# An attention, slot-expert and feed-forward kernel: a written order for the expert stage, and its constants loaded in parts over ScalarE's queue

## The chip, the cores and the metric

The program runs on one core of one Trainium2 chip. The metric is the device time of one execution in microseconds, lower is better. The times shown for the kernel before are the median and the ends of 3 runs. One further execution was profiled, and every row below comes from it.

## What is computed

Three layers in a chain, on 4 batches of 576 tokens with 512 features, all in float32:

```
attn = g * phi(q) M / (phi(q) z) + (1 - g) * softmax(causal(q k^T / 8)) v      # 8 heads of 64
logits = x @ phi                        # x = attn as 2304 x 512; 8 experts of 4 slots: 32 slots
d = softmax over the tokens(logits);  slot_input = d^T @ x
slot_out[e] = max(slot_input[e] @ w1[e], 0) @ w2[e]      # w1 512 x 1024, w2 1024 x 512, e = 0..7
y = softmax over the slots(logits) @ slot_out
out = (s * max(y @ w_in, 0)^2 + b) @ w_out               # w_in 512 x 2048, w_out 2048 x 512
```

The two arrays `w_in` and `w_out` arrive as float64 and are decoded on the chip.

## The kernel before, in words

**Attention.** 16 pairs of heads. What TensorE, ScalarE, VectorE and GpSimd do for them is one written order, the table `STEP`: each word is a part of a pair's work and the number of pairs it runs ahead. The first things that each pair needs are its keys (`load_keys`, L276) and its queries, values and memory (`load_rest`, L282). The scores are a matmul into PSUM (L308), the row maxima with the causal mask added are a VectorE instruction (L320 and L326), which reads the mask from the tile `cs`, and the exponentials are ScalarE's (L334). Transposes (L353) read the identity from `cs` as well. `cs` holds four things side by side: identity (128 columns), the mask for the first four blocks of rows (512), the mask for the last block (288), and a replication matrix `rep` (128), which is first read when the softmax over the tokens is finished. In each pair's iteration a piece of `w_in` is loaded into `raw` (L572) and decoded, the first step on ScalarE (L201).

**Loads.** All are issued by SyncE, in order. Eight semaphores serve them in turn, so each issue waits until the load eight places before has landed. `bet` (beta, from which ScalarE makes `eb` at L616 and L617 and VectorE `icst` at L620 and L623) and `cs` are among the first. Expert weights (33.5 MB) are loaded during the attention into all tiles that are free, as units of 512 columns, and into the tiles of the attention as it ends: `load_place`, `load_next`, and `used`, which refills a tile when its weights have been read.

**Experts.** Four experts stand in the 4 column groups of TensorE at once, so there are two halves, `a` = 0 and 1. `layer1(a)` multiplies the slots by `w1` (L664), takes the maximum with 0 on ScalarE into `hs` (L669), transposes it (L674) and copies it to `hT` (L220). `layer2(a)` multiplies by `w2` (L684) and copies to `so`. `slots_T(a)` transposes `so` (L697) into `sT`. `slot_softmax(b)` is the softmax over the slots for batch b: ten VectorE instructions and one of ScalarE (L744 to L753), five transposes (L758, L761) and two copies into `cT`. Its results `cex`, `chi` and `csk` stand in one buffer each for all batches. The tile `hs` lies in `raw64`, `hT` in `PT`, and `csk` in `F`; all three hold expert weights until these have been read. In this stage the framework's scheduler chooses the order on each engine.

**Feed-forward.** A written order again, `RAMP`, for the start: `g_piece` builds `slot_out @ w_in` (L789, L793, L797), `decode_part` decodes `w_out` (L201 to L209, L720, L722), `first` (L826 to L846) and `second` (L861) are the two matmuls with what lies between. Then follows the main loop.

Of the kernel before, what the change touches and what calls it, by code (L numbers as in the profile page):

```python
# [27 lines left out]
C_ID = 0  # L28
# [22 lines left out]
    kw=[0,0,0,0,0],  # L51
# [18 lines left out]
scl:2 U2.1:2 Wd:2 du:0 F1:3 pscl:2 C:1 A:1 E3.0:2 M:2 T0.1:3 T4.1:2 A4:1 U0.1:3  # L70
""".split()
# [19 lines left out]
def tile_attention_moe_ffn(  # L91
# [40 lines left out]
    ONCE = ("w1", "w2", "w3", "raw", "M", "x", "raw64", "F", "PT", "Q0", "Q1")  # L132
# [17 lines left out]
    wt, left = {}, []  # L150
# [13 lines left out]
    def load_place(n, tag):  # L164
# [4 lines left out]
        if n % 2 and (left or wkeys):  # L169
            if not left:  # L170
                left.extend([k] for k in wkeys.pop(-1 if tag == "x" else 0))
            keys.append(left.pop(0))
# [334 lines left out]
    def merge(part):  # L507
# [147 lines left out]
    hs, so = MB[:, 0:1024], MB[:, 1152:1664]  # L655
# [3 lines left out]
    def layer1(a):  # L659
        acc = [ps_y(), ps_y()]  # L660
        for kc in range(4):
            for fb in range(2):
                for j in range(4):
                    PE.matmul(  # L664
                        acc[fb][32 * j:32 * j + 32, :], slT[:, kc, :], wt["w1", a, kc, j, fb],
                        start=(kc == 0), stop=(kc == 3))
# [3 lines left out]
        for g in range(2):  # L670
            t = ps_h()
# [3 lines left out]
            evac(hT[a][:, 4 * g:4 * g + 4, :], t.rearrange("p (i s) -> p i s", i=4))  # L675

    def layer2(a):

        n = UNIT // (1 + a)
        acc = [ps_y() for _ in range(1 + a)]  # L680
        for fc in range(8):
            for i, y in enumerate(acc):
                for j in range(4):
                    last_pe[0] = PE.matmul(  # L684
# [4 lines left out]
        for i, y in enumerate(acc):  # L689
            evac(so[:, n * i:n * i + n], y[:, 0:n], ("a", "v")[i] if a else None)  # L690

    def slots_T(a):
        t = ps_h()
        if a:
            keep_warm(t, T["kw"][1])
        for dc in range(4):
            PE.transpose(t[:, dc * 128:(dc + 1) * 128], so[:, dc * 128:(dc + 1) * 128], ident)  # L697
        evac(sT[:, :, 16 * a:16 * a + 16].rearrange("p c (j s) -> p c j s", j=4),
             strided(t[:, 16 * a:16 * a + 1], (128, 4), (36, 4), (1, 4)), "v" if a else None)
# [28 lines left out]

    layer1(0)
    layer1(1)  # L730
    layer2(0)
    slots_T(0)
    load_out(0)

# [29 lines left out]
    for b in range(2):  # L764
        slot_softmax(b)
# [194 lines left out]
```

## Time and profile before

| | us |
|---|---|
| median of 3 runs | 511.17 |
| fastest and slowest of them | 508.05, 513.64 |
| the profiled execution | 512.23 |
| its span, first to last instruction | 510.4 |
| TensorE busy in it | 486.8 |

The profiled execution spends 1.8 us outside its span. All rows below are on the span's own clock, which begins with the first instruction. PE is TensorE's matmul, PEld its load of weights, DVE VectorE, ACT ScalarE, SPq SyncE's queue of issues. A float32 matmul stands in the trace as two records.

### The profile page before, as it was taken

How to read it: one execution, taken by the hardware profiler on the slowest of the kernel's cores; microseconds unless marked ns; L12 is line 12 of the kernel's file. 1: busy time of each engine (PE TensorE's matmuls, PEld its weight loads, DVE VectorE, ACT ScalarE, POOL GpSimd, SP SyncE). 2: the span in 40 equal slices, each digit the busy share in tenths (PEclk: the TensorE clock that was granted, in tenths of full speed). 3: DMA queues.
4: the chain of work that ended last, by engine and by line, in shares of the span. 5: the costliest groups of instructions: out<-in, count | busy, mean ns of one | idle time of the engine just before them, and what ended most of it. 6: DMA issues, size and time to landing. Idle time of an engine off the chain costs nothing.

```text
span 510.4 us, 8982 instructions
## 1 busy us (share of the span) xinstructions
PE 486.8 (95%) x3143; PEld 344.5 (67%) x3143; DVE 340.4 (67%) x934; ACT 334.3 (65%) x843; POOL 57.2 (11%) x73
## 2 busy tenths in 40 slices
PE   2999999999999999988998999999999999999997
PEld 1566665666566656763344667888888888888885
DVE  0888897888788878842226899984644655645451
ACT  2888876888788887720124799887766555566552
POOL 1122222222223312300000000000000000000000
PEclk9999999999999999998999999999999999999999
DMA  7689995344434442499997542500300100100101
GB/s 243 209 304 323 359 367 162 114 147 147 148 99 148 145 141 78 147 377 403 409 408 252 211 163 85 166 1 1 123 2 0 62 2 0 63 1 17 45 2 62
DMA packets 25821, 78.28 MB, mean 153 GB/s; under 512 B 3120, under 2 KB 3248, under 8 KB 25776
## 3 DMA queue, kind: packets, MB, share of 16 engines
q1 hardware_dynamic: 25776, 77.71, 43.7%
q8 instruction: 25, 0.41, 0.3%
q14 instruction: 20, 0.16, 0.1%
HBM read 69.84 MB, written 7.86 MB: 152 GB/s over the span
## 4 chain that ended last, share of the span: by engine, by line
PE 88%; DMA 6%; DVE 2%; ACT 2%; issue 1%; SPq 1%; DVEq 0%; ACTq 0%
PE y L861 39%; PE t L353 8%; PE o L402 8%; PE s L308 8%; PE s L312 3%; PE h L826 3%; PE s L373 3%; PE y L684 3%; DMA w<-in_w_dram 3%; PE t L356 2%; DMA cs<-in_cst_dram 2%; PE t L414 1%; DMA raw<-in_w_in_dram 1%; PE t L437 1%; PE t L450 1%; PE h L789 1%
## 5 line engine op out<-in xcount | busy, mean ns | idle before, releaser
L861 PE MATMUL y<-w,R 128*128 128x512 f32 x864 | 215.3, 393 | 0.7 <-ACT R L838 0.7
L861 PEld LDWEIGHTS y<-w,R 128*128 128x128 f32 x864 | 160.6, 188 | 37.1 <-issue 2.4
L830 ACT ACTIVATE P<-h 128x384 f32<-128x384 f32 x96 | 46.5, 485 | 55.1 <-PE h L826 54.8
L320 DVE CUSTOM_DVE_ANT_0 P<-s,cs 128x128 f32<-128x128 f32 (+3 forms) x128 | 58.3, 481 | 28.5 <-DMA cs<-in_cst_dram 11.2
L334 ACT ACTIVATE P<-P,st 128x128 f32<-128x128 f32 (+3 forms) x128 | 71.2, 557 | 0.4
L846 DVE TENSOR_TENSOR R<-P,R 128x384 fp32r<-128x384 f32 x47 | 26.1, 556 | 66.7 <-ACT R L844 66.6
L353 PE MATMUL t<-cs,P 128*128 128x128 f32 x320 | 54.2, 285 | 0.0
L353 PEld LDWEIGHTS t<-cs,P 128*128 128x128 f32 x320 | 34.8, 141 | 19.5 <-ACT P L334 6.3
L308 PE MATMUL s<-R,Q 64*128 64x128 f32 (+3 forms) x176 | 32.5, 476 | 10.8 <-DVE st L320 5.6
L222 ACT ACTIVATE PT<-t 128x256 f32<-128x256 f32 (+2 forms) x64 | 26.0, 433 | 13.8 <-PE t L353 13.8
L826 PE MATMUL h<-x,R 128*128 128x384 f32 x96 | 34.1, 356 | 0.5 <-DVE R L797 0.5
L836 ACT ACTIVATE P<-P,sbt 128x384 f32<-128x384 f32 x47 | 33.3, 708 | 1.4
L842 DVE SCALAR_TENSOR_TENSOR R<-P,sbt,R 128x384 fp32r<-128x384 f32 x49 | 30.1, 617 | 5.1 <-ACT R L838 2.1
L834 DVE SCALAR_TENSOR_TENSOR P<-P,sbt 128x384 f32<-128x384 f32 x49 | 29.9, 612 | 0.9 <-ACT P L830 0.9
L222 ACT ACTIVATE raw<-t 128x256 f32<-128x256 f32 (+2 forms) x64 | 25.8, 432 | 6.6 <-PE t L353 6.5
L308 PEld LDWEIGHTS s<-R,Q 64*128 64x128 f32 x176 | 15.5, 194 | 20.3 <-issue 10.6
L844 ACT ACTIVATE R<-P 128x384 fp32r<-128x384 f32 x47 | 24.6, 523 | 1.3
L832 ACT ACTIVATE P<-P 128x384 f32<-128x384 f32 x47 | 24.6, 523 | 1.3
L334 ACT ACTIVATION_READ_ACCUMULATOR P<-P,st 128x1 f32 x128 | 24.9, 195 | 0.0
L347 POOL TENSOR_SCALAR P<-P,st 128x576 f32<-128x576 f32 x16 | 16.1, 1008 | 65.0 <-DVE st L343 51.7
L826 PEld LDWEIGHTS h<-x,R 128*128 128x128 f32 x96 | 17.9, 188 | 6.3 <-DVE R L797 1.4
L431 POOL TENSOR_TENSOR x<-x,M 128x512 f32<-128x512 f32 x15 | 19.2, 1279 | 9.8 <-DVE x L425 8.6
(237 smaller groups left out, 748.7 us busy)
## 6 DMA issues: line engine op xcount, KB each, us to landing
w<-in_w_dram SPq DMA_DIRECT2D x38, 512.0 KB, 8.1
raw<-in_w_in_dram SPq DMA_DIRECT2D x16, 512.0 KB, 4.2
Q<-in_qvm_dram SPq DMA_DIRECT2D x10, 673.0 KB, 4.3
R<-in_qk_dram SPq DMA_DIRECT2D x32, 144.0 KB, 3.3
out_dram<-P SPq DMA_DIRECT2D x18, 256.0 KB, 2.0
PT<-in_w_out_dram SPq DMA_DIRECT2D x4, 1024.0 KB, 5.0
R<-in_qvm_dram SPq DMA_DIRECT2D x5, 673.0 KB, 4.4
wdr<-raw SPq DMA_DIRECT2D x12, 256.0 KB, 2.2
```

What stands on the lines that cost most here:

```text
L222: ACT.activation(out=dst, in_=src, func=AF.Copy)
L308: PE.matmul(ps[:, 512 * h:512 * h + n], q[r, t * 128:(t + 1) * 128], k[r, 0:n], start=True, stop=True)
L320: DVE.tensor_tensor_reduce(out=Pt[h, t], in0=x, in1=cs[:, C_M2 - n:C_M2], scale=-0.125, scalar=BIG, op0=ALU.add, op1=ALU.min, accum_out=st ...
L334: ACT.activation(out=pt, in_=pt, func=AF.Exp, scale=-1.0, bias=st[:, 18 + c:19 + c], accum_out=st[:, c:c + 1])
L353: PE.transpose(tp[:, kb * 128:(kb + 1) * 128], Pt[i, t][:, kb * 128:(kb + 1) * 128], ident)
L402: last_pe[0] = PE.matmul(o[64 * h:64 * h + 64, q0 - 64:512], lhs(kb, h), PTp[:, h, c:c + S - q0], start=(kb == 0), stop=(kb == 4))
L826: PE.matmul(g_t[n][2], G(k * 128, 128), cT[:, g * TG:(g + 1) * TG], start=True, stop=True)
L830: ACT.activation(out=r, in_=h, func=AF.Relu)
L834: DVE.scalar_tensor_tensor(out=r, in0=r, scalar=sbt[:, 0:1], in1=r, op0=ALU.mult, op1=ALU.mult)
L836: ACT.activation(out=r, in_=r, func=AF.Identity, scale=sbt[:, 0:1], bias=sbt[:, 1:2])
L842: DVE.scalar_tensor_tensor(out=lo, in0=r, scalar=sbt[:, 1:2], in1=hi, op0=ALU.add, op1=ALU.subtract)
L861: PE.matmul(acc[g, i], (hi, hi, lo)[j][:, c], (who, wlo, who)[j][k], start=(k == 0 and j == 0), stop=(k == NK - 1 and j == 2))
```

## The change

1. `bet` and `cs` are issued from ScalarE's queue, ahead of all else there, `cs` in four parts in this order: the last 128 columns of the first mask, the identity, the other 384 columns of that mask, the second mask. SyncE starts with the keys of pair 0. `phs`, `sbt` and the replication matrix are issued by SyncE at the end of the iteration before the first full one.
2. The expert stage has a written order for TensorE, ScalarE and VectorE, the table `EXPERTS`. A word is a part and its arguments: `1a.from.to` and `2a.from.to` are pieces of the two layers, `r` the maximum with 0, `h` the transposes (part 0) and the copies (part 1), `o` the copy of the second layer's result, `T` the slots' transposes, `c` the softmax (part 0 its VectorE and ScalarE instructions, part 1 transposes and copies), `w` the load of the first part of `w_out`.
3. The maximum with 0 is shared: ScalarE takes the first 512 columns, VectorE the others. The copies have named engines.
4. `hs` and `so` move to `R2`, which is no longer refilled with weights. The softmax of batch 1 has buffers of its own in the tile `raw`. The loads of half pairs are limited to six, so that the last weights stand in other tiles.
5. `keep_warm` calls with a count of 0 are removed.

```diff
-    load_keys(0)
-    load_rest(0)
-    SP.dma_start(out=cs, in_=cst)
-    SP.dma_start(out=bet, in_=beta)
-    SP.dma_start(out=phs, in_=phi)
-    SP.dma_start(out=sbt, in_=sb)
+    ACT.dma_start(out=bet, in_=beta)
+    for c in (slice(C_M2 - 128, C_M2), slice(C_ID, C_M1), slice(C_M1, C_M2 - 128), slice(C_M2, C_REP)):
+        ACT.dma_start(out=cs[:, c], in_=cst[:, c])
+    load_keys(0)
+    load_rest(0)
...
+            if i == -1:
+                SP.dma_start(out=phs, in_=phi)
+                SP.dma_start(out=sbt, in_=sb)
+                SP.dma_start(out=cs[:, C_REP:C_END], in_=cst[:, C_REP:C_END])
...
+EXPERTS = """
+10.0.4 11.0.1 r0 11.1.2 h0.0 11.2.4 h0.1 r1 c0.0 20.0.4 h1.0 h1.1 20.4.8 o0 c0.1 c1.0
+21.0.2 T0 21.2.4 c1.1 21.4.6 w0 21.6.8 o1
+""".split()
...
-    hs, so = MB[:, 0:1024], MB[:, 1152:1664]
+    RB = place("R2", SIZE["R2"])
+    hs, so = RB[:, 0:1024], RB[:, 1024:1536]
...
-        for fb in range(2):
-            ACT.activation(out=hs[:, fb * 512:(fb + 1) * 512], in_=acc[fb], func=AF.Relu)
+    def layer1_out(a):
+        ACT.activation(out=hs[:, 0:512], in_=acc1[a][0], func=AF.Relu)
+        DVE.tensor_scalar(out=hs[:, 512:1024], in0=acc1[a][1], scalar1=0.0, scalar2=-BIG, op0=ALU.max, op1=ALU.max)
...
-    layer1(0)
-    layer1(1)
-    layer2(0)
-    slots_T(0)
-    load_out(0)
...
-    for b in range(2):
-        slot_softmax(b)
-
-    layer2(1)
+    parts = {"1": layer1, "r": layer1_out, "h": hidden_T, "2": layer2, "o": layer2_out, "T": slots_T, "c": slot_softmax, "w": load_out}
+    with tc.manual_schedule(engines={mybir.EngineType.PE, mybir.EngineType.Activation, mybir.EngineType.DVE}):
+        for word in EXPERTS:
+            a = [int(i) for i in word[1:].split(".")]
+            if word[0] in "12":
+                a = [a[0], range(a[1], a[2])]
+            parts[word[0]](*a)
```

**ScalarE at the program's start.** Before, its first work is the load of the function table and the two exponentials of `bet`:

```order
L616 ACT_TABLE_LOAD
L616 ACTIVATE eb<-bet 128x12
L617 ACTIVATE eb<-bet 128x12
L334 ACTIVATE P,st<-P,st 128x128
L290 ACTIVATE F<-F 128x576
```

Now five issues of loads stand ahead of these:

```order
L615 DMA bet<-in_beta_dram 128x12
L617 DMA cs<-in_cst_dram 128x128 x2
L617 DMA cs<-in_cst_dram 128x384
L617 DMA cs<-in_cst_dram 128x288
L622 ACT_TABLE_LOAD
L622 ACTIVATE eb<-bet 128x12
```

The loads went from SyncE's queue to ScalarE's, and what ScalarE computes stands behind them. On VectorE the nine small instructions on `eb` and `icst` now stand ahead of the first maximum instead of behind it.

**TensorE from the end of layer 1 to the begin of layer 2.** `y<-...,slT` is layer 1, `h<-cs,...` transposes of `hs`, `y<-...,PT` layer 2 of the first half. Before:

```order
L664 MATMUL y<-PT,slT 32x512 x2
L674 MATMUL h<-cs,raw_2788 128x128 x8
L664 MATMUL y<-PT,slT 32x512 x2
L664 MATMUL y<-P,slT 32x512
L664 MATMUL y<-PT,slT 32x512 x2
L664 MATMUL y<-R_2660,slT 32x512
L664 MATMUL y<-P,slT 32x512
L674 MATMUL h<-cs,raw_2788 128x128 x4
L684 MATMUL y<-P,PT 32x512
L674 MATMUL h<-cs,raw_2788 128x128 x4
L684 MATMUL y<-P,PT 32x512
```

Now:

```order
L696 MATMUL h<-cs,R_2792 128x128 x8
L678 MATMUL y<-raw_2569,slT 32x512 x2
L678 MATMUL y<-Q_2574,slT 32x512
L678 MATMUL y<-PT,slT 32x512
L678 MATMUL y<-raw_2569,slT 32x512 x2
L678 MATMUL y<-Q_2574,slT 32x512
L678 MATMUL y<-PT,slT 32x512 x4
L678 MATMUL y<-P,slT 32x512
L678 MATMUL y<-PT,slT 32x512 x2
L678 MATMUL y<-R_2664,slT 32x512
L678 MATMUL y<-P,slT 32x512
L708 MATMUL y<-P,PT 32x512 x2
```

The first half's transposes stand half of `layer1(1)` earlier, and the second half's, which stood between the first two matmuls of layer 2, come 16 matmuls later.

**VectorE before the transposes of batch 1.** `x<-h` copies the transposed softmax of batch 0, `raw` and `raw_2790` are the buffers of batch 1 and of batch 2. It now has this stretch, up to the two last rows, which finish what the transposes of batch 1 read:

```order
L231 CAST x<-h 128x512 [waits DMAHW3_49,DMAHW2_49,PE_49]
L775 TENSOR_REDUCE raw<-lgs 128x5 [waits DMAHW6_49,DMAHW5_49,DMAHW4_49]
L783 CAST F<-raw_2790 128x10x32 [waits DVE_49,PE_49]
L776 TENSOR_TENSOR raw<-lgs,raw 128x160 [waits DVE_49]
L784 TENSOR_TENSOR F<-raw_2790 128x10x32
L778 TENSOR_REDUCE raw<-raw 128x5 [waits Activation_49]
L776 TENSOR_TENSOR raw_2790<-lgs,raw_2790 128x160 [waits DVE_49]
L779 TENSOR_SCALAR raw<-raw 128x5 [waits DVE_49]
L780 RECIPROCAL raw<-raw 128x5 [waits DVE_49]
L781 TENSOR_TENSOR raw<-raw 128x160 [waits DVE_49]
```

```order
L778 TENSOR_REDUCE raw_2790<-raw_2790 128x5 [waits Activation_49]
L782 CAST raw<-raw 128x160 [waits DVE_49]
L779 TENSOR_SCALAR raw_2790<-raw_2790 128x5 [waits DVE_49]
L783 CAST raw<-raw 128x10x32 [waits DVE_49]
L784 TENSOR_TENSOR raw<-raw 128x10x32
```

Between the copy for batch 0 and the last instruction for batch 1 stand 14 instructions, of which five belong to batch 2. Before, batch 1 shared its buffers with batch 0, and its last two instructions on `F` could only follow the transposes of batch 0.

## Rows read from the trace of the kernel before

**Rows 1.** The page's chain that ended last, share of the span by engine.

```profile
PE 88%; DMA 6%; DVE 2%; ACT 2%; issue 1%; SPq 1%; DVEq 0%; ACTq 0%
```

**Rows 2.** That chain in order of time: start us, us, what.

```profile
3.08 7.95 DMA cs<-in_cst_dram
...
71.02 7.24 DMA raw<-in_w_in_dram
```

**Rows 3.** Timeline of the start: start us, us, engine, line, what [idle before, releaser].

```profile
0.73 1.28 ACT L616 ACT_TABLE_LOAD   x1 [0.73 <-PEq L950]
...
3.08 0.43 SPq L610 DMA_DIRECT2D cs<-in_cst_dram  x1
...
5.24 1.66 PE L308 MATMUL s<-R,Q 64*128 64x128 f32 x8 [5.24 <-DMA Q<-in_qvm_dram]
...
8.88 0.33 SPq L572 DMA_DIRECT2D raw<-in_w_in_dram  x1
...
11.17 0.29 DVE L320 CUSTOM_DVE_ANT_0 P<-s,cs 128x128 f32<-128x128 f32 x1 [11.17 <-DMA cs<-in_cst_dram]
11.31 0.21 ACT L616 ACTIVATE eb<-bet 128x12 f32<-128x12 f32 x1 [9.29 <-DMA bet<-in_beta_dram]
...
17.24 0.68 ACT L201 ACTIVATE win<-raw 128x512 f32<-128x512 f32 x1
```

**Rows 4.** Windows of the start: busy us per engine; last PEclk, DMA share, GB/s.

```profile
2.00:4.00 2.00, 0.00 (x0) 0.00 (x0) 0.00 (x0) 0.01 (x1) 0.00 (x0) 1.00 0.81 205
4.00:6.00 2.00, 0.77 (x6) 0.80 (x8) 0.00 (x0) 0.00 (x0) 0.67 (x1) 1.00 0.95 322
6.00:8.00 2.00, 0.89 (x5) 0.17 (x2) 0.00 (x0) 0.00 (x0) 0.00 (x0) 1.00 1.04 309
8.00:10.00 2.00, 0.00 (x0) 0.00 (x0) 0.00 (x0) 0.00 (x0) 0.00 (x0) 1.00 0.97 373
10.00:12.00 2.00, 0.26 (x2) 0.26 (x4) 0.83 (x7) 0.59 (x3) 0.00 (x0) 1.00 0.92 244
```

**Rows 5.** Timeline of the expert stage, TensorE and ScalarE.

```profile
236.86 8.77 PE L664 MATMUL y<-w,slT 128*32 128x512 f32 x64 [0.45 <-DVE slT L650]
...
247.17 0.13 PEld L664 LDWEIGHTS y<-w,slT 128*32 128x32 f32 x4 [0.30 <-issue]
247.60 0.13 PEld L664 LDWEIGHTS y<-w,slT 128*32 128x32 f32 x4 [0.30 <-issue]
...
250.87 1.09 ACT L669 ACTIVATE raw<-y 128x512 f32<-128x512 f32 x2 [17.24 <-DMA w<-in_w_dram]
...
254.65 0.59 ACT L220 COPY PT<-h 128x512 f32<-128x512 f32 x1
...
265.38 0.66 PE L697 MATMUL h<-cs,raw 128*128 128x128 f32 x4 [0.27 <-ACT raw L220]
...
266.60 4.73 PE L684 MATMUL y<-w,PT 128*32 128x256 f32 x82
...
274.71 0.38 ACT L222 ACTIVATE raw<-y 128x256 f32<-128x256 f32 x1 [0.28 <-PE y L684]
...
276.30 0.64 PE L789 MATMUL y<-win,raw 128*32 128x128 f32 x16 [0.32 <-DVE raw L224]
```

**Rows 6.** Timeline of VectorE, first and last of nine softmax instructions in a row.

```profile
266.71 0.49 DVE L752 COPY F<-raw 128x320 f32<-128x320 f32 x1 [8.40 <-PE h L761]
...
269.50 0.25 DVE L751 CAST raw<-raw 128x160 fp32r<-128x160 f32 x1
```

**Rows 7.** Windows of the expert stage, columns as in rows 4 (third busy time is VectorE's).

```profile
236.00:240.00 4.00, 3.55 (x24) 1.24 (x27) 0.29 (x1) 0.00 (x0) 0.00 (x0) 0.71 1.03 405
268.00:272.00 4.00, 4.00 (x80) 2.71 (x77) 1.56 (x6) 0.33 (x1) 0.00 (x0) 1.00 1.00 384
272.00:276.00 4.00, 3.51 (x34) 1.58 (x25) 1.90 (x6) 2.37 (x6) 0.00 (x0) 1.00 0.12 46
280.00:284.00 4.00, 3.35 (x15) 2.83 (x16) 3.93 (x10) 3.29 (x6) 0.00 (x0) 1.00 1.04 404
```

More of the change, by code (lines that the diff above doesn't have):

```diff
@@ L50 @@
     sim=0,
-    kw=[0,0,0,0,0],
     sb=[30, 34],
@@ L149, in tile_attention_moe_ffn @@
     at = {k: i for i, k in enumerate(k for pair in wkeys for k in pair)}
-    wt, left = {}, []
+    wt, left, odd = {}, [], [6]
     def load_units(keys, dst):
@@ L168, in load_place @@
         keys = [wkeys.pop(0) for _ in range(min(n // 2, len(wkeys)))]
-        if n % 2 and (left or wkeys):
+        if n % 2 and odd[0]:
+            odd[0] -= 1
             if not left:
-                left.extend([k] for k in wkeys.pop(-1 if tag == "x" else 0))
+                left.extend([k] for k in wkeys.pop(0))
             keys.append(left.pop(0))
@@ L654, in tile_attention_moe_ffn, with layer1 @@
     HB = place("PT", SIZE["PT"])
-    hs, so = MB[:, 0:1024], MB[:, 1152:1664]
+    RB = place("R2", SIZE["R2"])
+    hs, so = RB[:, 0:1024], RB[:, 1024:1536]
     sT = MB[:, 1024:1152].rearrange("p (c s) -> p c s", c=4)
     hT = [HB[:, 1024 * i:1024 * i + 1024].rearrange("p (f s) -> p f s", f=8) for i in range(2)]
-    def layer1(a):
-        acc = [ps_y(), ps_y()]
-        for kc in range(4):
+    acc1, acc2 = {}, {}
+    def layer1(a, kcs):
+        if a not in acc1:
+            acc1[a] = [ps_y(), ps_y()]
+        for kc in kcs:
             for fb in range(2):
@@ L674, in layer1, with layer2 @@
                 PE.transpose(t[:, i * 128:(i + 1) * 128], strided(hs[:, c:c + 1], (2, 128)), ident)
-            evac(hT[a][:, 4 * g:4 * g + 4, :], t.rearrange("p (i s) -> p i s", i=4))
-    def layer2(a):
+    h_t = {}
+    def layer2(a, fcs):
         n = UNIT // (1 + a)
-        acc = [ps_y() for _ in range(1 + a)]
-        for fc in range(8):
-            for i, y in enumerate(acc):
+        if a not in acc2:
+            acc2[a] = [ps_y() for _ in range(1 + a)]
+        for fc in fcs:
+            for i, y in enumerate(acc2[a]):
                 for j in range(4):
-                    last_pe[0] = PE.matmul(
+                    PE.matmul(
                         y[32 * j:32 * j + 32, 0:n], hT[a][:, fc, 32 * j:32 * j + 32],
@@ L688, in layer2, with layer2_out @@
                 used(8)
-        for i, y in enumerate(acc):
-            evac(so[:, n * i:n * i + n], y[:, 0:n], ("a", "v")[i] if a else None)
+    def layer2_out(a):
+        n = UNIT // (1 + a)
+        for i, y in enumerate(acc2[a]):
+            evac(so[:, n * i:n * i + n], y[:, 0:n], "av"[i])
     def slots_T(a):
         t = ps_h()
-        if a:
-            keep_warm(t, T["kw"][1])
         for dc in range(4):
@@ L727, in decode_out, with slot_softmax @@
         load_out(k2 + 2)
-    layer1(0)
-    layer1(1)
-    layer2(0)
-    slots_T(0)
-    load_out(0)
     XC = place("x", SIZE["x"], F32R)
     cT = XC
-    csk = place("F", SIZE["F"]).rearrange("p (t r s) -> p t r s", t=5, r=4)
-    c5 = MB[:, 1984:1994]
-    cex, chi = (MB[:, 1664 + 160 * i:1824 + 160 * i].rearrange("p (t s) -> p t s", t=5) for i in range(2))
-    chi = chi.bitcast(F32R)
-    def slot_softmax(b):
+    CB = place("raw", SIZE["raw"])
+    csks = [place("F", SIZE["F"]), CB[:, 0:640]]
+    cexs = [MB[:, 1664:1994], CB[:, 640:970]]
+    def slot_softmax(b, part, by="va"):
+        i = b % 2 if b < 2 else 0
+        csk = csks[i].rearrange("p (t r s) -> p t r s", t=5, r=4)
+        if part:
+            t, t2 = ps_h(), ps_h()
+            for i in range(4):
+                PE.transpose(t[:, i * 128:(i + 1) * 128], csk[:, i].rearrange("p r s -> p (r s)"), ident)
+            PE.transpose(t2[:, 0:64], csk[0:64, 4].rearrange("p r s -> p (r s)"), ident[0:64, 0:64])
+            evac(cT[:, b * S:b * S + 512], t, by[0])
+            evac(cT[:, b * S + 512:(b + 1) * S], t2[:, 0:64], by[1])
+            return
+        c5 = cexs[i][:, 320:330]
+        cex, chi = (cexs[i][:, 160 * r:160 * r + 160].rearrange("p (t s) -> p t s", t=5) for r in range(2))
+        chi = chi.bitcast(F32R)
         DVE.tensor_reduce(out=c5[:, 0:5], in_=lgs[:, b], axis=AX.X, op=ALU.max)
@@ L786, in g_piece @@
         if part == 0:
-            keep_warm(t, T["kw"][2] if i == 0 else 0)
             for dc in range(4):
```

30 lines of the change are left out of this document (13 added, 17 removed).

## The prediction

> **What bounds the kernel now.** I read the chain that ended last first, since it says whose time is worth anything. TensorE has 88% of it and loads 6% [rows 1]; so an edit pays where the chain leaves TensorE, or where TensorE's own order leaves it idle. In order of time the chain leaves it first at the very start: from 3.08 us, for 7.95 us, it is the load of the constants [rows 2]. The timeline there shows why: pair 0's scores begin at 5.24, the first maximum only at 11.17, freed by that load, and the exponential of `bet` stands 9.29 us for its own [rows 3]. Then I went to the two stages that the change reorders. Between 236.86, where layer 1 begins, and 276.30, where the first window matmul of the feed-forward begins, lie 39.4 us [rows 5].
>
> **Term 1, the constants at the start.** Nothing is computed less; loads change queue and order. Before the first maximum the changed kernel needs pair 0's keys and queries, the first 128 columns of mask, and nine small VectorE instructions on `eb`, which wait for ScalarE. ScalarE: five issues at 0.43 us, the price of one on SyncE's queue [rows 3], from 0.73 make 2.9; the table load of 1.28 makes 4.2; two exponentials at 0.21 make 4.6. The nine small ones, narrower than the softmax instructions of rows 6 (0.34 each) and by estimate half as long, end near 6.0 [rows 6]. This is hidden by the queries if these come later, and costs little if not.
>
> The queries landed for 5.24 with nothing beside them but SyncE's loads. Now 481 KB from ScalarE's queue (128 rows of 128 + 128 + 384 + 288 + 12 words) may go ahead of them; at 322 GB/s [rows 4] that is 1.5 us at most. So scores begin between 5.24 and 6.7. The first two of their eight records take 0.4 us of 1.66 [rows 3]. First maximum between 5.7 and 7.2; I take 6.9, near the late end, as the engines that move data are already 81 to 95% busy in this stretch [rows 4]. It stood at 11.17, so the start moves by 4.3 us, at best by 5.5.
>
> The other end comes from how late a landing is told. By bytes, the constants (541 KB, behind 984 KB of keys, queries and values) had passed by 7.5 us: 0.41 MB by 4, 1.05 by 6, 1.67 by 8 [rows 4]. VectorE was freed at 11.17, 3.6 us later. If such a lag falls on pair 0's queries or the first mask, the first maximum stands at 10.4 and the gain is 0.8.
>
> What is late next: the first piece of `w_in`, which ScalarE reads at 17.24 without a wait that shows [rows 3]. Its 524 KB follow 2.58 MB of the loads ahead of it. 2.91 MB had passed by 12 [rows 4], and the other 0.2 MB take 0.8 us at 244 GB/s, so by bytes it ended near 12.8, and with the lag of 3.6 near 16.4. Now 131 KB less stand ahead (the replication matrix and `phs` are moved behind), 0.5 us. It then lands between 12.3 and 15.9, and is wanted at 17.24 less 4.3, 12.9. The middle is 14.1, so ScalarE may stand 1.2 us with exponentials queued behind it, for which TensorE's transposes wait. I take 0.5 of it as lost, for scores of the next pair stand ahead of those transposes. **Term 1: 3.8 us gained, bounds 0.8 and 5.5.**
>
> The Trainium skill ("Trainium Kernel Development and Optimization", section Key Constraints) says that loads issued from several queues run on the same 16 engines and interleave, and that a second queue only saves issue time. By that rule the gain from the queue itself is SyncE's issues alone, and the constants would cost the queries the whole 1.5 us. The busy share of 0.95 [rows 4] agrees; what is left is the order of need.
>
> The three loads put into SyncE's queue two pairs later (130 KB) are issues of 0.43 us each beside work that does not need them.
>
> **Term 2, the expert stage.** TensorE's work is the same; I add it up in the written order. A group of four records of 512 columns starts every 0.43 us [rows 5], so 0.1075 each: 128 records of layer 1 are 13.8, 64 of `layer2(0)` 6.9. 256 columns cost 4.73 / 82 = 0.058, with its end; steady 0.0535, half of 0.1075: 128 records are 6.9. Four transposes are 0.66 [rows 5]; two sets of eight, three sets of four and two single ones make 5.0. The first 64 records take 8.77 where 6.9 would do [rows 5], as the granted clock is 0.71 there, a mean of a part at 1.2 and a part at 2.4 GHz [rows 7]; what precedes is unchanged, so the 1.9 stay. Sum 34.5.
>
> Then the waits. The maximum with 0, which stood 17.24 us because `hs` lay in a tile of weights [rows 5], now finds `R2` free after the first quarter of `layer1(1)`, beside TensorE's next 16 records: hidden. The copy into `PT` must still wait for the last of layer 1, as `PT` holds its weights; 0.59 for it [rows 5] and 0.1 for passing on, 0.7 on the path. The new wait is `c1.1`: its transposes need 14 VectorE instructions behind the copy for batch 0. Nine such took 3.04 us, 266.71 to 269.75 [rows 6], so 14 take 4.7. The copy for batch 0 (0.6) starts as its four transposes end, so the buffer is ready 5.3 us after these. TensorE meanwhile has one single transpose (0.2), `21.0.2`, `T0` and `21.2.4`: 0.2 + 1.7 + 0.7 + 1.7 = 4.3. With the passing on it stands about 1.2. Queued behind is all that is left of layer 2, 3.4 us, and nothing fills the gap.
>
> 34.5 + 0.7 + 1.2 = 36.4 from 236.86: layer 2 ends at 273.3, against 274.71 when ScalarE copies its result [rows 5]: 1.4 gained. After it two copies now start together, where VectorE's came later, as it was at work on a softmax: 0.2 more. **Term 2: 1.6 us, bounds 0** (the wait at `c1.1` grows to 2.8, as VectorE's chain passes through ScalarE twice) **and 2.8** (it is hidden).
>
> The weights bound it next. The load engines are full to 272 and idle after it [rows 7]; the last 2 MB they move are `w_out` and a window, 5 us at 384 to 405 GB/s, so the last weights land by 267, and the new order wants them from 271. Hidden, unless the wait at `c1.1` goes: then the margin is under 3.
>
> **Term 3, the ramp.** Six softmax instructions of batch 2 that stood behind the expert stage are now inside it. VectorE is busy 3.93 of 4 us at 280 [rows 7]; six at 0.34 are 2.0, of which I take 0.5, since TensorE waits for VectorE there only now and then. **Bounds 0 and 0.9.** The `keep_warm` calls had a count of 0: nothing.
>
> **Sum.** 3.8 + 1.6 + 0.5 = 5.9. The profiled execution took 512.23: 506.3. The median of the runs is 1.06 lower, which would give 505.3. I take 505.8, between them.
>
> **The rivals.**
>
> - *The start gains little.* The lag of 3.6 us falls on the queries or the mask: term 1 is 0.8, time 508.8. For it: the lag is there in the trace, of a cause that no row shows. Against: the queries themselves came without it, 0.59 MB with the keys by 5.24 [rows 3].
> - *VectorE is in time at `c1.1`, and `w_in` is not late.* 1.2 and 0.5 more: 504.1. For it: five of the 14 instructions fill pauses of dependent ones, so the mean from rows 6 may be high. Against: the nine that it comes from were mixed in the same way.
> - *The start's gain is spent later.* The chain hangs for 7.24 us on a load of `w_in` at 71.02 [rows 2], while the engines that load are full. If that load's landing is fixed by bytes since the start, the 3.8 turn into a longer wait: 509.6. Against: each such issue waits for a buffer that the engines free, so the stream moves with them.
> - *Slower: the clock falls at the new wait.* TensorE stands at `c1.1`, and the ramp behind has its own gaps. If the granted clock falls there to 1.2 GHz and stays through the ramp, to 292, some 22 us in which TensorE is busy about half at its limit cost 11: 517. It decides from a loss of 5.9 us of full-speed work; the dip at 236 [rows 7] cost 1.9. Against: 272 to 276, with half a microsecond of pauses, were granted 1.00 [rows 7].
>
> The Trainium skill ("TensorE: Matmul & The Clock Gate", section "HAM oscillation — how this bites in real kernels") tells of a matmul kernel that lost the clock at each wait for data; by that rule this rival is the result. Only the 0.71 at 236 [rows 7] speaks for it here.
>
> **How the numbers follow.** Forecast 0.60; little at the start 0.15; in time at `c1.1` 0.12; spent later 0.08; slower 0.05. The bounds of the terms are 0.8 and 9.2 gained; from 511.17 that is 510.4 and 502.0, and the forecast's own part 503.5 to 507.5. The range, 501.8 to 510.5, spans these; it leaves out the slower rival and some 0.1 for what is larger at the start than its bounds. About 1%, 5.1 us, is what a measurement here can tell: below 506.1 lie 0.42 of the forecast's 0.60, all of the second rival and a little of the others: faster 0.57, same 0.38, slower 0.05.
>
> **What would show it.** First maximum at 6.9 and no wait for constants; ScalarE's first read of `raw` near 13.5 with a wait for its load; from layer 1 to the first window matmul 37.8 us instead of 39.4, with a wait of TensorE of about 1.2 for VectorE at the transposes of batch 1; the granted clock at 1.00 after it. It is wrong if the first maximum stands later than 9, if the stretch from 60 to 82 grew, or if layer 2 stands still for weights.

## The result and the profile after

The changed kernel took 507.09 us (median of 7 runs, 502.12 to 509.79), the kernel before 511.35 beside it (7 runs, 508.05 to 513.64): a ratio of 0.989, 95% interval 0.985 to 0.994. In a second set of runs (the tenth experiment) it was 0.993 (0.990 to 0.996). The medians are of all runs and the ratios of the fast ones alone: one of these 7 runs, and four of the 12 in the second set, were over 1.5% above the fastest and count as slow. The forecast was 505.8. The profiled execution of the changed kernel took 506.75, with a span of 504.9, 5.5 less than before.

The page has the chain by engine, which answers to [rows 1]:

```profile
PE 91%; DMA 4%; DVE 2%; ACT 1%; issue 0%; SPq 0%; DVEq 0%; ACTq 0%
```

The chain in order of time leaves TensorE for loads at these three places only; the constants and the `raw` of [rows 2] are gone from it. Through the last two TensorE is busy all the same, so only the first is a pause:

```profile
1.97 3.86 DMA Q<-in_qvm_dram
...
240.24 9.34 DMA w<-in_w_dram
...
252.16 7.66 DMA P<-in_w_dram
```

The timeline of the start, for [rows 3] (start us, us, engine, line, what):

```profile
1.14 2.01 ACTq L617 DMA_DIRECT2D cs<-in_cst_dram  x4
3.18 1.28 ACT L622 ACT_TABLE_LOAD   x1 [3.18 <-issue]
4.47 0.21 ACT L622 ACTIVATE eb<-bet 128x12 f32<-128x12 f32 x1
...
5.41 0.44 SPq L578 DMA_DIRECT2D raw<-in_w_in_dram  x1
...
5.96 3.06 PE L315 MATMUL s<-R,Q 64*128 64x128 f32 x12 [5.96 <-DMA Q<-in_qvm_dram]
...
6.80 0.29 DVE L327 CUSTOM_DVE_ANT_0 P<-s,cs 128x128 f32<-128x128 f32 x1 [1.11 <-PE s L315]
...
12.87 0.67 ACT L208 ACTIVATE win<-raw 128x512 f32<-128x512 f32 x1
```

The first maximum stands at 6.80 instead of 11.17 and waits for TensorE's scores, not for the constants; the scores wait for the load of the queries. ScalarE reads the first piece of `w_in` at 12.87 without a wait. The expert stage, for [rows 5], on three engines:

```profile
232.00 9.37 PE L678 MATMUL y<-w,slT 128*32 128x512 f32 x64 [0.45 <-DVE slT L660]
...
243.16 0.60 ACT L684 ACTIVATE R<-y 128x512 f32<-128x512 f32 x1 [15.15 <-PE y L678]
...
249.56 0.60 ACT L229 ACTIVATE PT<-h 128x512 f32<-128x512 f32 x1 [5.80 <-DMA w<-in_w_dram]
250.21 0.62 PE L708 MATMUL y<-P,PT 128*32 128x512 f32 x2 [0.68 <-ACT PT L229]
...
259.81 0.31 DVE L775 TENSOR_REDUCE raw<-lgs 128x5 f32<-128x160 f32 x1
...
261.75 1.93 PE L708 MATMUL y<-w,PT 128*32 128x256 f32 x32
...
263.18 0.48 DVE L784 TENSOR_TENSOR raw<-raw 128x320 f32<-128x320 f32 x1
...
263.81 0.63 PE L767 MATMUL h<-cs,raw 128*128 128x128 f32 x4
...
267.92 0.38 ACT L229 ACTIVATE R<-y 128x256 f32<-128x256 f32 x1 [3.03 <-PE y L708]
268.30 0.42 DVE L231 COPY R<-y 128x256 f32<-128x256 f32 x1 [3.13 <-PE y L708]
269.53 0.64 PE L815 MATMUL y<-win,raw 128*32 128x128 f32 x16 [0.32 <-DVE raw L231]
```

From layer 1 (232.00) to the first window matmul (269.53) it is 37.5 us instead of 39.4. The maximum with 0 runs at 243.16, in the middle of layer 1, where it stood until 250.87. The windows, for [rows 7] (busy us by engine; last the granted clock, DMA share, GB/s):

```profile
228.00:232.00 4.00, 2.33 (x11) 1.99 (x11) 1.57 (x5) 0.01 (x1) 0.00 (x0) 0.73 1.03 402
232.00:236.00 4.00, 4.00 (x20) 0.99 (x24) 0.00 (x0) 0.00 (x0) 0.00 (x0) 0.50 0.88 348
236.00:240.00 4.00, 4.00 (x40) 1.13 (x36) 0.00 (x0) 0.00 (x0) 0.00 (x0) 0.92 0.89 301
...
268.00:272.00 4.00, 2.90 (x32) 1.59 (x26) 2.88 (x7) 2.41 (x7) 0.00 (x0) 1.00 0.73 246
272.00:276.00 4.00, 2.91 (x15) 1.86 (x15) 3.51 (x8) 3.23 (x7) 0.00 (x0) 0.78 1.03 386
276.00:280.00 4.00, 4.00 (x16) 3.27 (x15) 2.95 (x6) 1.87 (x4) 0.00 (x0) 0.80 0.48 194
```

The granted clock falls to 0.50 (1.2 GHz) ahead of layer 1, and part of two windows behind the stage is at that level as well.

The 5.5 us come about so: the shift against the kernel before is 4.4 at the first maximum and 5.6 from pair 7 on, 4.9 at layer 1, 6.8 at the first window matmul, and 5.5 from 286 us to the end.

### The profile page after: what moved, and what is told of

The parts are those of the page before. It is cut to its first block, busy times and chain, and to the rows that moved or that the text cites. A ratio compares the mean times of both kernels' runs of the same rounds, so it can differ in the third digit from the quotient of the medians.

```text
span 504.9 us, 8984 instructions
## 1 busy us (share of the span) xinstructions
PE 487.1 (96%) x3143; PEld 344.9 (68%) x3143; DVE 343.0 (68%) x939; ACT 331.6 (66%) x838; POOL 57.4 (11%) x73
## 4 chain that ended last, share of the span: by engine, by line
PE 91%; DMA 4%; DVE 2%; ACT 1%; issue 0%; SPq 0%; DVEq 0%; ACTq 0%
PE y L885 40%; PE s L315 8%; PE t L360 8%; PE o L409 8%; PE s L319 4%; PE s L380 4%; PE h L851 3%; DMA w<-in_w_dram 2%; PE t L363 2%; PE t L421 2%; PE y L678 2%; DMA P<-in_w_dram 2%; PE t L444 1%; PE t L457 1%; PE y L708 1%; PE t L404 1%
## 5 line engine op out<-in xcount | busy, mean ns | idle before, releaser
L871 DVE TENSOR_TENSOR R<-P,R 128x384 fp32r<-128x384 f32 x47 | 26.1, 556 | 66.4 <-ACT R L869 66.3
L327 DVE CUSTOM_DVE_ANT_0 P<-s,cs 128x128 f32<-128x128 f32 (+3 forms) x128 | 58.3, 480 | 18.8 <-ACT PT L229 9.0
```

Source lines behind the costliest of these rows:

```text
L327: DVE.tensor_tensor_reduce(out=Pt[h, t], in0=x, in1=cs[:, C_M2 - n:C_M2], scale=-0.125, scalar=BIG, op0=ALU.add, op1=ALU.min, accum_out=st ...
```

## The experiments

Each ran beside the kernel before, on the same chip as it. A ratio is to that kernel, with its 95% interval. Where times in one execution are compared, they are starts read from the timelines: the first maximum of a pair, the first record of layer 1, the first window matmul.

| kernel | median us | ratio | interval |
|---|---|---|---|
| start alone | 509.88 | 0.998 | 0.995 to 1.001 |
| start alone, again | 508.30 | 0.995 | 0.994 to 0.997 |
| experts alone | 508.09 | 0.996 | 0.995 to 0.998 |
| changed kernel, again | 508.51 | 0.993 | 0.990 to 0.996 |
| scheduler's order | 508.72 | 0.996 | 0.993 to 0.998 |
| pauses filled | 506.33 | 0.991 | 0.989 to 0.993 |
| one queue | 510.74 | 1.000 | 0.997 to 1.003 |
| weights spread | 514.01 | 1.005 | 1.003 to 1.007 |
| weights spread, pauses filled | 513.13 | 1.003 | 1.002 to 1.005 |
| weights behind `raw` | 506.89 | 0.991 | 0.987 to 0.994 |
| weights behind `raw`, pauses filled | 507.08 | 0.990 | 0.986 to 0.994 |

| execution | first maximum | pair 2 | pair 7 | layer 1 | first window matmul |
|---|---|---|---|---|---|
| before | 11.17 | 28.67 | 94.98 | 236.86 | 276.30 |
| before, again | 9.15 | 27.47 | 92.90 | 234.83 | 274.02 |
| experts alone (old start) | 8.84 | 27.10 | 94.63 | 236.51 | 273.44 |
| changed | 6.80 | 24.36 | 89.34 | 232.00 | 269.53 |
| changed, again | 8.18 | 25.34 | 90.90 | 232.87 | 269.81 |
| start alone | 7.38 | 24.46 | 92.76 | 234.68 | 274.11 |
| start alone, again | 7.67 | 24.74 | 90.83 | 232.75 | 272.19 |
| pauses filled | 7.20 | 24.61 | 90.75 | 233.02 | 270.73 |
| scheduler's order | 8.36 | 26.11 | 91.48 | 234.00 | 272.35 |
| one queue | 7.58 | 29.20 | 95.37 | 237.35 | 273.00 |
| weights spread | 7.28 | 24.73 | 89.73 | 239.60 | 277.11 |
| weights behind `raw` | 8.58 | 26.32 | 91.32 | 233.89 | 270.92 |

**The start alone.** The kernel before with this part of the diff only:

```diff
+    ACT.dma_start(out=bet, in_=beta)
+    for c in (slice(C_M2 - 128, C_M2), slice(C_ID, C_M1), slice(C_M1, C_M2 - 128), slice(C_M2, C_REP)):
+        ACT.dma_start(out=cs[:, c], in_=cst[:, c])
     load_keys(0)
```

> The kernel before with the constants' part of the change alone (ScalarE's queue, four parts, order of need, the other three loads two pairs later). Theory A, the shift made at the start is kept and the stretch from 71 to 79 us gains another 1.3 because the same loads come earlier against what waits for them: first maximum at 6.8, shift against the kernel before 4.4 up to 70 us and 5.6 behind 80 us, expert stage unchanged at 39.4, time 505.5 to 506.5 where the kernel before has 511.2. Theory B, the 1.3 came from the other places of the weights (limit of half pairs), which this kernel does not have: shift 4.4 throughout, time 507 or, if the wait at 71 us grows, 508 to 509.

The first maximum came at 7.38, but of a shift of 4.7 at pair 1 only 2.2 was left at pair 7. The waits from 20 to 97 us (engine, line, for what: us in total, times, longest) tell where it went:

```profile
ACT raw L201 <- DMA raw<-in_w_in_dram: 5.0, 2, 3.2
ACT win L201 <- DMA raw<-in_w_in_dram: 3.6, 2, 3.0
```

ScalarE waits for pieces of `w_in`, with the exponentials behind it. Neither theory held as it was put: the shift grew nowhere, and it did not stay at 4.4. It was run a second time to see whether that is the rule.

> The constants' part alone, once more, since in its first execution 2.5 of the 4.7 us gained at the start went again at ScalarE's waits for raw, 17.0 us for the iteration of pair 6. Theory A, such a loss is the rule while the weights are issued beside these loads: first maximum at 6.8 to 8.6, pair 7 at 91 to 93 (before: 92.9 and 95.0), the iterations of pairs 1 to 6 together 1 us or more above the undisturbed 74.9 (9.9, 12.56, 12.45, 12.45, 12.88, 14.65), ratio 0.995 to 0.999. Theory B, it was one bad draw: pair 7 at 89 to 90.5, ratio 0.992 to 0.994, as much as the start's shift.

The same two rows of the second execution:

```profile
ACT raw L201 <- DMA raw<-in_w_in_dram: 3.4, 2, 2.0
ACT win L201 <- DMA raw<-in_w_in_dram: 1.0, 2, 0.8
```

Pair 7 began at 90.83, 0.2 ahead of theory A's range; the iterations of pairs 1 to 6 took 1.1 more than undisturbed, and the part alone gained 0.5% instead of 0.2%: theory A in the main, with much chance in it. The order of SyncE's issues up to pair 6 is the same in this kernel and in the changed one, so their different waits for `raw` are differences between executions. Nor does the loss come with the new start: from pair 2 to pair 7 it is 66.4 us on the average of the three executions with the old start, and 66.1 of the six with the new one and unspread weights (both of the start alone and of the changed kernel, pauses filled, scheduler's order), where undisturbed iterations make 65.0.

**The old start once more.** The kernel before, unaltered.

> The kernel before once more, for its start. Theory A, the first maximum at 11.17 was a late landing of that one execution: it stands at 8.5 to 10 here (8.84 in the one other execution with the old start), and the first iterations are as much longer, so that pair 7 begins at 94.5 to 95.5 as in the other two. Theory B, 11.17 is the rule and 8.84 the exception: 10.5 to 11.5.

First maximum 9.15, pair 7 at 92.90: the first as in theory A, the second earlier than it said. The 11.17 on which the prediction rests was the latest of three.

**The experts alone.** The changed kernel with the loads of the old start.

```diff
-    ACT.dma_start(out=bet, in_=beta)
...
     load_keys(0)
     load_rest(0)
+    SP.dma_start(out=cs, in_=cst)
+    SP.dma_start(out=bet, in_=beta)
```

> The changed kernel with the start of the kernel before. Theory A, the expert part is worth what its stage lost, 1.5 to 1.9 us, where the granted clock does not take some back behind it: first maximum at 11.2, layer 1 to first window matmul 37.5 to 38.0 instead of 39.4, time 509.3 to 510. Theory B, what the stage gains the ramp gives back, since there TensorE has to wait for VectorE or runs at the lower clock: stage 37.5, but s0's nine records take 3.9 instead of 2.3, time 511, no difference. Theory C, the load wait at 71 to 79 us is shortened by this part: shift of 1.3 at 80 us already, time 508.

The stage took 36.9 (273.44 less 236.51), and the ratio of 0.996 makes 1.8 us: theory A in size, with more in the stage and a loss behind it as in theory B. At pair 7 the shift was 0.4, so theory C falls. From the first window matmul to the nineteenth record of the first products with `w_out` it was 12.9 us, against 11.6 in the kernel before's execution, with the granted clock low in between.

**The scheduler's order.** The same code in the same sequence, but the framework sets the order on each engine.

```diff
-    with tc.manual_schedule(engines={mybir.EngineType.PE, mybir.EngineType.Activation, mybir.EngineType.DVE}):
-        for word in EXPERTS:
+    for word in EXPERTS:
...
```

> The changed kernel with the expert stage's code in the same order, but with the framework's scheduler setting the order on each engine. Against the written order it puts the transposes of batch 1 (c1.1) 24 records, 1.3 us, earlier on TensorE, and on VectorE the first copy to PT and the maximum with 0 behind eight softmax instructions of batch 0. Theory A, in the written order VectorE finishes with batch 1 just as TensorE comes to its transposes, with no slack: 1.3 us earlier TensorE waits 1.0 to 1.4 for VectorE, and the time is 0.5 to 1.4 above the changed kernel's. Theory B, VectorE has slack there or the clock gives it back: no wait above 0.3, same time. Theory C, the written order itself is what the stage gained and the new buffers nothing: stage 39 or more.

TensorE's timeline ahead of the transposes of batch 1:

```profile
263.32 0.66 PE L722 MATMUL h<-cs,R 128*128 128x128 f32 x4
263.90 1.06 PE L708 MATMUL y<-w,PT 128*32 128x256 f32 x8
264.89 0.66 PE L767 MATMUL h<-cs,raw 128*128 128x128 f32 x4
```

Eight records of 256 columns take 0.99 until the transposes begin, where 0.0535 each would make 0.43. That is no wait: the row is busy for 1.06, past the begin of the transposes, and VectorE had finished with batch 1 long before, as the scheduler changed its order too:

```profile
259.63 0.48 DVE L784 TENSOR_TENSOR raw<-raw 128x320 f32<-128x320 f32 x1
```

The records start two at a time, where in the written order they start four at a time. Two windows of 0.8 us in this stretch, of this kernel and of the changed one, have 9 and 17 records:

```profile
263.90:264.70 0.80, 0.80 (x9) 0.38 (x8) 0.73 (x5) 0.00 (x0) 0.00 (x0) 1.00 1.03 410
```

```profile
261.75:262.55 0.80, 0.80 (x17) 0.54 (x20) 0.73 (x5) 0.32 (x1) 0.00 (x0) 1.00 1.02 410
```

So theory A's wait is not there, and the loss has another cause: layer 2 took 18.3 us against 17.6 in the written order (252.37 to 270.70, and 250.21 to 267.85), so the order is worth 0.7 there. Of the whole time it shows nothing, as the intervals overlap. From the first record of layer 1 to the first of layer 2 it is 18.2 to 18.4 in both kernels with new buffers and 19.1 before. With a stage of 38.4, theory C falls. That it is `hs` in a tile without weights, and not the shared maximum, is likely, as the wait of 17.24 [rows 5] is gone, but not shown alone.

**TensorE's pauses filled.** Matmuls of 64 columns on the identity, of which this is the first place:

```diff
     t = ps_h()
+    keep_warm(t, 4)
     for kc in range(4):
         PE.matmul(t[:, kc * 32:(kc + 1) * 32], uacc[:, kc * 128:(kc + 1) * 128], sel, start=True, stop=True)
```

> The changed kernel with short matmuls on the identity put into TensorE's pauses: four ahead of the matmul of the slots' input, one ahead of layer 1, one each ahead of the second slots' transposes, of the first and third window matmul and of the first feed-forward matmul, two ahead of the first product with w_out. Their results are overwritten. Theory A, the granted clock falls because TensorE pauses: filled, it stays at 1.00 from 228 to 240 and from 272 to 280, the slots' input takes 1.05 instead of 1.81, the first 64 records of layer 1 6.9 to 7.5 instead of 9.2, the nine records of s0 2.3 instead of 3.9: 3 to 4 us gained in all, time 503 to 504.5. Theory B, the fall has another cause than these pauses: the same 0.73, 0.50 and 0.78, time 507 to 508, as the added matmuls cost up to 1 us.

The windows ahead of layer 1 and behind the stage:

```profile
232.00:236.00 4.00, 3.80 (x24) 1.47 (x27) 0.29 (x1) 0.00 (x0) 0.00 (x0) 0.60 1.04 408
236.00:240.00 4.00, 4.00 (x40) 1.08 (x36) 0.00 (x0) 0.00 (x0) 0.00 (x0) 0.97 0.82 300
...
272.00:276.00 4.00, 3.30 (x25) 2.22 (x24) 3.63 (x8) 2.78 (x7) 0.00 (x0) 1.00 0.99 391
276.00:280.00 4.00, 4.00 (x19) 3.33 (x18) 3.59 (x8) 2.69 (x5) 0.00 (x0) 1.00 0.80 322
```

Behind the stage the clock stayed at 1.00, and it did so in all three executions with filled pauses (this one and the two below); of eleven without, it fell there in seven. Ahead of layer 1 it fell all the same. The ratio of 0.991 lies inside the interval of the changed kernel's own: the gain in time is not shown. One of the added matmuls did harm. The one meant for the second slots' transposes, which come behind layer 2, stands in the trace in the middle of it, behind two records that start one at a time:

```profile
264.87 0.62 PE L711 MATMUL y<-w,PT 128*32 128x256 f32 x2
265.42 0.43 PE L223 MATMUL h<-cs 128*128 128x64 f32 x2
265.78 0.42 PE L711 MATMUL y<-w,PT 128*32 128x256 f32 x4
```

From its first record to its last, layer 2 took 18.6 here, and 18.8 in the two other executions with filled pauses, against 17.6 in the changed kernel and 17.8 with the weights behind `raw`. Most of the 1.3 that the clock gives back is lost there. Even without filling the same kernel can do either: the kernel before kept 1.00 in its first execution and not in its second, and the lines of that second one are these:

```profile
276.00:280.00 4.00, 2.88 (x15) 1.76 (x16) 3.94 (x9) 2.74 (x6) 0.00 (x0) 0.84 1.03 398
280.00:284.00 4.00, 4.00 (x15) 3.27 (x14) 3.01 (x7) 1.98 (x4) 0.00 (x0) 0.73 0.60 241
```

**One queue.** The constants in the same parts, on SyncE's queue.

```diff
-    ACT.dma_start(out=bet, in_=beta)
...
     load_keys(0)
+    SP.dma_start(out=cs[:, C_M2 - 128:C_M2], in_=cst[:, C_M2 - 128:C_M2])
     load_rest(0)
+    SP.dma_start(out=bet, in_=beta)
+    for c in (slice(C_ID, C_M1), slice(C_M1, C_M2 - 128), slice(C_M2, C_REP)):
+        SP.dma_start(out=cs[:, c], in_=cst[:, c])
```

> The changed kernel with the constants in the same parts, but on SyncE's queue: the keys, the first part of the mask, queries and the rest of pair 0, beta, the other three parts, then pair 1. Theory A, the order of need is what counts and not the queue: first maximum at 6.5 to 8.4 as with ScalarE's queue (6.8 to 8.4 in four executions), time within 0.3% of the changed kernel's. Theory B, the queue itself counts: the issues of 0.43 us each, one behind the other, put pair 1's queries and the first piece of w_in 2 us later, and ScalarE waits for raw at 13 to 15 us, 1 to 2 us lost.

The first maximum came at 7.58, no later than with ScalarE's queue, but pair 2 at 29.20 instead of 24.4 to 26.3. The chain in order of time, ScalarE's timeline and a window show the mechanism:

```profile
7.57 8.05 DMA raw<-in_w_in_dram
```

```profile
15.64 0.66 ACT L208 ACTIVATE win<-raw 128x512 f32<-128x512 f32 x1 [2.85 <-DMA raw<-in_w_in_dram]
```

```profile
16.00:20.00 4.00, 1.83 (x5) 0.76 (x6) 2.93 (x11) 3.39 (x11) 1.34 (x3) 0.58 0.63 184
20.00:24.00 4.00, 4.00 (x22) 4.00 (x22) 1.30 (x5) 2.69 (x8) 0.93 (x1) 0.56 0.57 165
```

The first piece of `w_in` was issued at 7.57 instead of 5.41 and landed 8.05 us later. ScalarE stood 2.85 for it with exponentials behind, TensorE ran dry, and its granted clock fell to 0.58. The iteration of pair 1 took 14.4 us instead of 9.9, and over ten runs nothing was left of the changed kernel's gain (a ratio of 1.000). So theory B for the time, at more than twice its price, though the first maximum came as theory A has it. The Trainium skill ("Trainium Kernel Development and Optimization", section Key Constraints) says that a second queue saves the time of issuing and no more; the trace agrees, as the issue came 2.2 us later, but that is not a small thing where an engine stands behind the load.

**The weights spread.** Instead of all by 67 us, two tiles of expert weights per iteration from the fourth on, SyncE in the written order.

```diff
-        for _ in range(0 if p < 6 else 2):
+        for _ in range(2 if 3 <= p < 13 else 0):
             load_next()
...
-    with tc.manual_schedule(engines={mybir.EngineType.PE, mybir.EngineType.Activation, mybir.EngineType.DVE, mybir.EngineType.Pool}):
+        with tc.manual_schedule(engines=four | ({mybir.EngineType.SP} if part[0] == first else set())):
```

> The changed kernel with its expert weights issued later: two tiles in each iteration from the fourth on, in the written order on SyncE's queue, where they were all issued by 67 us; the places that are loaded as the attention ends are Q1, F, PT, raw64 instead of raw64, F, Q1, PT. Theory A, what the start gains is lost again at ScalarE's waits for raw, because the loads of w_in share the engines with the weights until 74 us: with the weights spread there is no wait for raw beyond 0.3 us, the iterations of pairs 1, 3, 5 and 6 last the same as the undisturbed ones (12.45 to 12.9, the first of a batch 14.44), the first maximum of pair 7 stands at 88.5 to 89.5 for a first maximum of 7, and the time is 503.5 to 506. Theory B, the waits for raw have their cause in the landings, not in the other load: they stay, 507. Theory C, the later weights are missing in the expert stage: layer 1 or 2 stands still, above 508.

Up to pair 7 it is theory A: after pair 0 the iterations took 9.95, 12.56, 12.46, 12.45, 12.89 and 14.65, none longer than undisturbed. Then each of the next eight lost about a microsecond; the waits from 20 to 230 us:

```profile
ACT raw L208 <- DMA raw<-in_w_in_dram: 15.1, 6, 3.1
```

So other loads beside `raw` are what makes ScalarE wait, but the spread only moved them: the weights now stood between the queries and the next keys, with `raw` behind. The version with the pauses filled as well, run beside it, lost the same way.

> The changed kernel with both the weights spread and the short matmuls in TensorE's pauses (results overwritten). If both effects are real and independent, as I hold: no wait for raw beyond 0.3 us, the granted clock at 1.00 behind the expert stage, below 1.00 for at most 3.5 us ahead of layer 1, time 502.5 to 504.5, below both kernels. If the clock's gain is only luck of one execution: as the spread alone. If the weights are late: above 507.

**The weights right behind `raw`.** One word of `STEP` moved, from behind the queries to behind the load of `raw`.

```diff
-D2.0:2 T4.0:1 T3.1:1 E0.0:2 U4.1:1 E1.1:2 T3.0:1 D2.1:2 U3.1:1 U4.0:1 S4:2 U3.0:1 T0.0:2 LG:2 P:0
+D2.0:2 T4.0:1 T3.1:1 E0.0:2 U4.1:1 E1.1:2 T3.0:1 D2.1:2 U3.1:1 U4.0:1 S4:2 U3.0:1 T0.0:2 LG:2 LW:-1 P:0
...
-Wa:2 T2.0:2 B:0 E2.1:2 D3.1:2 R:4 F0:3 LW:-1 E4.0:2 E3.1:2 dx:0 D3.0:2 T1.0:2 D0.0:3 de:0 O0:1 Wb:2
+Wa:2 T2.0:2 B:0 E2.1:2 D3.1:2 R:4 F0:3 E4.0:2 E3.1:2 dx:0 D3.0:2 T1.0:2 D0.0:3 de:0 O0:1 Wb:2
```

> As the spread weights, but the two weight loads of an iteration stand right behind the load of raw on SyncE's queue, and no longer between the queries and the next keys. Theory A, what cost a microsecond in each of the pairs 7 to 14 was the order within the iteration, keys and raw behind one megabyte of weights: all iterations from pair 2 on undisturbed (12.3 to 14.65), pair 7 at 89 to 90.5, layer 1 at 232 to 233.5, no wait for raw beyond 0.5, time 505.5 to 507.5, 0.5 to 2 below the changed kernel in this call. Theory B, any weights beside a load of w_in cost ScalarE a wait: iterations of 13 and more again, 512.

Theory A: from pair 2 on every iteration was undisturbed (12.28 to 14.65, pair 6 14.65), and the waits from 20 to 97 us hold none for `raw`. Pair 7 (91.32) and layer 1 (233.89) came later than it says, as the first maximum did (8.58). The shares of the load engines in 40 slices of the span, of the changed kernel and of this one:

```profile
DMA  8899983444344443599999433300300100100001
```

```profile
DMA  8343447566746764899999533300300100100001
```

The first is full for six slices and idle by half until the expert stage; the second spends that half. The ratio was 0.991, the changed kernel's beside it 0.993.

> The same with the short matmuls in TensorE's pauses (results overwritten). If the granted clock falls behind the expert stage for want of TensorE work, as I hold: 1.00 from 268 to 290, and 1 to 1.5 us below the spread without them, 504.5 to 506; below 1.00 for 3 to 4 us ahead of layer 1 as before. If those pauses are not the cause: the same time as the spread without them or 0.3 more.

Here the clock stayed at 1.00 behind the stage, as theory A has it, and the time was that of the version without the matmuls (507.08 and 506.89). It decides nothing: in the profiled execution of that version the clock was at 1.00 there as well, without filling, and the matmul inside layer 2 costs 0.9.

**The changed kernel once more.**

> The changed kernel once more, unaltered, beside the other two. Theory A, its profiled execution was a good draw: first maximum at 6.8 to 8.4, some wait for raw in the iterations of pairs 1 and 6, pair 7 at 89.5 to 91.5 instead of 89.34; the stage from layer 1 to the first window matmul 37 to 38; the granted clock low once behind the expert stage or not at all, as its fall depends on where the pauses fall; median 507 to 508.5, ratio 0.992 to 0.995. Theory B, 89.34 is the rule, and the median 506 to 507.

Theory A. The first maximum came at 8.18 and pair 7 at 90.90, the clock fell behind the stage, and the ratio was 0.993. Three versions (pauses filled, weights behind `raw`, both) have ratios of 0.990 and 0.991, between the two of the changed kernel (0.989 and 0.993). Their intervals overlap its own, so that they beat it is not shown.

## Why the prediction was right, and where it was not

**The constants.** The mechanism was right: with the order of need, the maximum no longer waits for constants, but for scores. The size was not, at both ends of the difference. "It stood at 11.17" was one landing out of three (11.17, 9.15, 8.84). The prediction saw that lag of 3.6 us behind the bytes, and used it as a bound; it should have asked whether the lag would be there in the next execution. And 6.80, which meets the forecast of 6.9, was luck: it is the earliest of ten executions with the constants on ScalarE's queue, which go to 8.6, with 7.8 as their mean, and eight of them lie beyond the upper bound of 7.2. All ten wait for scores, and these for the queries, as in the latest of them (weights behind `raw`):

```profile
7.73 1.65 PE L315 MATMUL s<-R,Q 64*128 64x128 f32 x8 [7.73 <-DMA Q<-in_qvm_dram]
...
8.58 0.29 DVE L327 CUSTOM_DVE_ANT_0 P<-s,cs 128x128 f32<-128x128 f32 x1 [2.87 <-PE s L315]
```

The scores began at 5.96 to 7.73, and at 5.24 to 5.57 with the old start. So the step that failed is "scores begin between 5.24 and 6.7": with the constants beside them the queries come up to 2.5 us later, not 1.5 at most, and six of the ten lie beyond 6.7. On the average of the three and the six executions named above, the shift is 2.1 at the first maximum, where 4.3 was forecast, 2.8 at pair 2 and 3.2 at pair 7 (94.2 and 91.0). So 3.2 us reach the main part, where 3.8 was forecast, but about 1 of them arises behind the first maximum, and no run tells where from. Timed alone the part gave 1.0 and 2.4 of 510.6 and 510.8.

**The first piece of `w_in`.** The feared wait of 1.2 at 12.9 did not come: ScalarE read it at 12.87 at once, and in no execution with the constants on ScalarE's queue did it stand more than 0.23 for it. It was real all the same. One queue brought it with 2.85 us, and with the clock it made that iteration 4.5 longer.

**"The start's gain is spent later."** This rival had 0.08. Its place was right, ScalarE's waits for `raw` up to pair 7, and so was its cause, the loads that share the engines: with the weights placed behind `raw` there is no wait. But the gain is not spent there. In the start alone these waits took 2.5 of 4.7 us, and in the changed kernel's profiled execution the same place gave 1.3 more; on the average the stretch from pair 2 to pair 7 costs the same with either start (66.4 and 66.1). Its argument against, that the stream of loads moves with the buffers, held: the last weights ahead of pair 7 were issued at 71.8 before and at 67.2 in the changed kernel.

**The expert stage.** 37.8 forecast, 37.5 measured, by other terms. Two more executions with the written order and all else as in the changed kernel (its second, experts alone) took 36.9, three more with the old order 39.2 to 39.4, so the stage is worth about 2.2 and not 1.6. The wait at `c1.1` was put at 1.2 and was 0.1: 32 records begin at 261.75, end by 263.5 with 0.0535 each and 263.7 by the modelled end, and the transposes start at 263.81. The step that failed was the 0.34 for each of VectorE's 14 instructions [rows 6]. The prediction held that the nine it comes from were mixed in the same way; they were in small part, and those of 160 columns stand 0.35 to 0.37 apart from start to start. Two batches mixed took 3.85 (259.81 to 263.66), 0.275 each, and where the next belongs to the other batch, such an instruction is followed after 0.23. The rival with VectorE in time there (0.12) had that right. There is no slack: VectorE and TensorE's records end together. The two copies after layer 2 were to start together and gain 0.2; they started at 267.92 and 268.30, as the second half's last product ends later, and the 0.2 did not come. Against these, the first 64 records took 9.37, not 8.77, as the clock was lower. That the clock is what they lose by shows in the execution of the one queue, the only one of fourteen whose clock stayed at 1.00 there: 7.07. The 0.7 for the copy into `PT` came as put (0.68).

**The ramp.** Forecast 0.5 gained, measured 1.3 lost from the first window matmul to 286 us. The step that failed is that VectorE's 2.0 us less would be worth 0.5 to TensorE. Without the low clock they bring 0.1: 11.5 us from the first window matmul to the nineteenth record with weights behind `raw`, 11.6 before. The first nine records took 3.91 at the lower clock, where the kernel before had 2.34.

**"Slower: the clock falls."** It fell, not at the new wait, which is not there, but at the pauses behind the stage, and it cost 1.3, not 11. The step that failed was "stays through the ramp, to 292": by 280 it was back at 1.00. The Trainium skill ("TensorE: Matmul & The Clock Gate", section "HAM oscillation — how this bites in real kernels") describes a matmul kernel whose clock goes at each wait for data. The window of the one queue at 16, with TensorE behind a load, agrees (0.58). The pauses at 272 are shorter ones for VectorE and ScalarE, and in four of eleven executions they left the clock at 1.00. Whether the new stage makes the fall more frequent (six of seven executions, against one of four with the old stage) stays open.

**The sum.** Forecast 5.9: 3.8, 1.6 and 0.5. By the ratios it was 5.4 in the first set and 3.8 in the second. The profiled executions differ by 5.5, but this is a late draw at the start before and an early one after, less what the lower clock took ahead of layer 1 and behind the stage. By the parts it is start 1.0 to 3.2 and experts 1.8. So that the sum came near is in part luck: the start brought less than forecast, the stage more, and the ramp took away what it should have added.

## What to carry to other kernels

A gain read off one profiled execution at a load's landing is the difference to one draw: look at the start of several executions before sizing it. A row of TensorE that is long for its count need not hold a wait: see how many records start at a time. A load that the busiest engines wait for late belongs ahead of the bulk loads in the queue, and bulk loads for tiles that are free from the start should go where the load engines idle, right behind the urgent ones; here that took the waits away, but a gain in time over the changed kernel is not shown. What a small wait costs is set by what stands behind it in that engine's order: 2.85 us of ScalarE became 4.5 of the kernel.

## What the runs showed of the hardware

- The same loads from the same queue freed VectorE at 8.84, 9.15 and 11.17 us in three executions. With the constants on a second queue the queries let the scores begin at 5.96 to 7.73 in ten, and at 5.24 to 5.57 with the constants behind them in three.
- The granted clock behind the expert stage was 1.00 in one execution of the kernel before and 0.84 and 0.73 in two windows of another, at the same instructions; this alone is 1.3 us of 511.
- Eight records of 256 columns that start two at a time took as long as sixteen that start four at a time (9 and 17 records in 0.8 us, with one of the work before).
- One megabyte of weights ahead of the keys and `raw` in the queue cost about 1 us in each iteration; behind `raw` it cost none.
